# Segment sums of the opening taken by TensorE, and the layernorm of the w2 stage taken from accumulated sums and squares

## The chip, the cores and the metric

One core of a Trainium2 chip. The time is the device time of one execution in microseconds (us). A "profiled span" comes from the trace of one execution and is about 1.7 us below that execution's device time. TensorE is PE in the profile, its weight load PEld, VectorE DVE, ScalarE ACT, GpSimd POOL, SyncE SP.

## The reference, cut to what matters

```python
mod = (_silu(c) @ w_mod).reshape(1, 6, 1, -1)
sa, ca, ga, sb, cb, gb = ...                           # six vectors of 1024
h = _layernorm(x) * (1 + ca) + sa                      # x: 2048 x 1024
x = x + ga * _A_ref(h, mem0, Wq, Wk, Wv, Wo, 32)       # 64 segments of 32 rows, with a memory of 8 rows
h = _layernorm(x) * (1 + cb) + sb                      # called u in the kernel
# _B_ref(u):
g  = shifted(_gelu(_layernorm(u) @ w1))
x1 = u + g @ w2                                        # called x1b
h2 = _gelu(_layernorm(x1) @ w3) @ w4                   # the layernorm of x1 is called z
return x + gb * (x1 + h2)
```

The kernel estimates the memories of all segments from segment means (`hbar`: the sum over each segment of `h`, for the first one with the memory rows, over 40), and checks the estimate later.

## The kernel before

The opening: a tile of 128 rows is normalised (statistics on DVE, `xn` on POOL), transposed by PE into PSUM (`pt`), and evicted with scale and shift into `hh`, most of it by ACT. DVE then sums each segment out of `hh`.

```python
hsum = sb1.tile([P, KT, NSEG], F32, name="hsum")
def ln1_pair(tp_):                     # two tiles of 128 rows
    ...
    xn = xnp.tile([P, D], BF16, name="xn")                          # 3 buffers
    nc.gpsimd.tensor_scalar(xn[:], xt[:], rstd, nmr[:], ALU.mult, ALU.add)
    for kt in range(KT):
        nc.tensor.transpose(pt[:, kt, i * P:(i + 1) * P], xn[:, kt * P:(kt + 1) * P], ident[:])
    ...                                # hh = pt * (1 + ca) + sa, on DVE and ACT
    def seg_sum(s0, ns, col):
        nc.vector.tensor_reduce(hsum[:, :, s0:s0 + ns], hh[...], AX.X, ALU.add)
    ...
def g_prep():
    nc.vector.tensor_reduce(msum[:], hh[:, :, C_M0:C_M0 + M], AX.X, ALU.add)
    nc.vector.tensor_add(hsum[:, :, 0], hsum[:, :, 0], msum[:])
    nc.vector.tensor_scalar(gs["hbar"][:], hsum[:], 1.0 / (M + SEG), None, ALU.mult)
```

The w2 stage: 16 tiles of 128 rows. The tile's sum goes to memory and, normalised as `z`, through a transposing transfer into `z2a` (tiles 0 to 7) or `z2b` (8 to 15), which the w3 stage reads.

```python
def ln_act(smp, dst, src):             # bn_stats x2, bn_aggr, ve on DVE; rstd on POOL
    mean, rstd = layernorm_stats(smp, src)
    nc.vector.scalar_tensor_tensor(nmr[:], mean, -1.0, rstd, ALU.mult, ALU.mult)
    nc.scalar.activation(dst, src, ACT.Identity, bias=nmr[:], scale=rstd)
def Ba(t):
    ...
    for n2 in range(2):
        ...                            # 8 products into acc
        nc.vector.tensor_tensor(x1b[:, cs], acc[:], u[:, cs], ALU.add)
    nc.scalar.dma_start(x1b_d[ts, :], x1b[:])
    ln_act(bsm, z[:], x1b[:])
for i, u in enumerate(lagged(Ba, Bb, list(range(NTT)), lag=1)):    # Bb(t): transpose z of tile t
    u()
    ...
    if i == 14:                        # Winograd sums of z2a ("zs") and of the first w3 block ("ring")
        for f in z_sums(0):
            keep_order(f())
        w3_sums(0, keep_order)
```

A scheduler sets the order of the instructions on each engine; `keep_order` pins one behind what stands before it in the program.

Of the kernel before, what the change touches and what calls it, by code (L numbers as in the profile page):

```python
# [9 lines left out]
BF16 = mybir.dt.bfloat16  # L10
F32 = mybir.dt.float32
F16 = mybir.dt.float16
I32 = mybir.dt.int32
ACT = mybir.ActivationFunctionType
ALU = mybir.AluOpType
AX = mybir.AxisListType
# [3 lines left out]
P = 128  # L20
S = 2048
D = 1024
KT = D // P
H = 32
DH = 128
M = 8
SEG = 32
NSEG = S // SEG
# [5 lines left out]
EPS = 1e-5  # L34
# [26 lines left out]
def kernel(ctx, tc, A_x, A_mem0, A_Wq, A_Wk, A_Wv, A_Wo, A_seg_len, B_x, B_w1, B_w2, B_w3, B_w4, c, w_mod, out,  # L61
           dbg=None, force_fallback=False, no_fallback=False):
    nc = tc.nc
# [29 lines left out]
    mhalf = const.tile([P, 1], F32, name="mhalf")  # L93
    nc.vector.memset(mhalf[:], -0.5)

    saT = const.tile([P, KT], F32, name="saT")
    ca1T = const.tile([P, KT], F32, name="ca1T")
# [69 lines left out]
    def first_pass(late_hook):  # L167
# [134 lines left out]
        hh = hpool.tile([P, KT, MAIN + CONV + 1], BF16, name="hh")  # L302
        C_T0, C_M0, C_T1, C_MEM = MAIN, MAIN + 32, MAIN + 40, MAIN + 136
# [37 lines left out]
        sm = ph.enter_context(tc.tile_pool(name="ph1_sm", bufs=4, side="right"))  # L341
        sb1 = ph.enter_context(tc.tile_pool(name="ph1_sb", bufs=1, side="right"))
        pst = ph.enter_context(tc.tile_pool(name="ph1_pst", bufs=2, space=PSUM))
        wst = ph.enter_context(tc.tile_pool(name="ph1_w", bufs=6, side="right"))
        ps1 = ph.enter_context(tc.tile_pool(name="ph1_ps1", bufs=1, space=PSUM))
# [7 lines left out]
        LN_ORDER = list(range(1, NTT)) + [0]  # L353
        xts = []

        def load_x(eng, i):
            xt = xp.tile([P, D], BF16, name="xt")
            xts.append(xt)
            ins = []
            for rows, toks in p_rows(LN_ORDER[i]):  # L360
                ins.append(eng.dma_start(xt[rows, :], x2[toks, :]))
            return ins
# [13 lines left out]
        small_ps = ps1.tile([P, 512], F32, name="small_ps")  # L376
# [9 lines left out]
        for half in range(2):  # L386
            for j in range(KT):
                for kt in range(KT):
                    nc.tensor.matmul(pm[:, half * KT + j:half * KT + j + 1], lhsT=wms[half * 2 + j // 4][:, kt, (j % 4) * P:(j % 4 + 1) * P], rhs=scT[:, kt:kt + 1],
                                     start=(kt == 0), stop=(kt == KT - 1))  # L390
        nc.vector.tensor_copy(saT[:], pm[:, 0:KT])
        nc.vector.tensor_scalar(ca1T[:], pm[:, KT:2 * KT], 1.0, None, ALU.add)
        hsum = sb1.tile([P, KT, NSEG], F32, name="hsum")

        def ln1_pair(tp_):
            def f():
                pt = pst.tile([P, KT, 2 * P], BF16, name="pt")
                for i in range(2):
                    t = 2 * tp_ + i
                    xt = xts[t]  # L400
                    mean, rstd = layernorm_stats(sm, xt[:])
                    nm = sm.tile([P, 1], F32, name="ln_nm")
                    nc.vector.tensor_scalar(nm[:], mean, -1.0, None, ALU.mult)
                    nmr = sm.tile([P, 1], F32, name="ln_nmr")
                    nc.gpsimd.tensor_tensor(nmr[:], nm[:], rstd, ALU.mult)
                    xn = xnp.tile([P, D], BF16, name="xn")
                    nc.gpsimd.tensor_scalar(xn[:], xt[:], rstd, nmr[:], ALU.mult, ALU.add)
                    if t + 8 < NTT:
                        load_x(nc.gpsimd, t + 8)
                    for kt in range(KT):  # L410
                        nc.tensor.transpose(pt[:, kt, i * P:(i + 1) * P], xn[:, kt * P:(kt + 1) * P], ident[:])
                c0 = 2 * P * tp_
                pieces = [(c0, 0, 2 * P)] if tp_ < 7 else [(c0, 0, P + 32), (C_T1, P + 32, 96)]
                ndve = 4 if tp_ < 2 else 1
                for kt in range(KT):
                    for col, o, n in pieces:
                        dst = hh[:, kt, col:col + n]
                        src = pt[:, kt, o:o + n]
                        if kt < ndve:
                            nc.vector.tensor_scalar(dst, src, ca1T[:, kt:kt + 1], saT[:, kt:kt + 1], ALU.mult, ALU.add)  # L420
                        else:
                            nc.scalar.activation(dst, src, ACT.Identity, bias=saT[:, kt:kt + 1], scale=ca1T[:, kt:kt + 1])

                def seg_sum(s0, ns, col):
                    nc.vector.tensor_reduce(hsum[:, :, s0:s0 + ns], hh[:, :, col:col + ns * SEG].rearrange("p k (s j) -> p k s j", j=SEG), AX.X, ALU.add)
                if tp_ < 7:
                    seg_sum(1 + 8 * tp_, 8, c0)
                else:
                    seg_sum(57, 4, c0)
                    seg_sum(0, 1, C_T0)  # L430
                    seg_sum(61, 3, C_T1)
            return f

        def w0_unit(hp, hl, which, i):
# [11 lines left out]
        gs = {}  # L446

        def g_prep():
            msum = sb1.tile([P, KT], F32, name="msum")
            nc.vector.tensor_reduce(msum[:], hh[:, :, C_M0:C_M0 + M], AX.X, ALU.add)  # L450
            nc.vector.tensor_add(hsum[:, :, 0], hsum[:, :, 0], msum[:])
            gs["hbar"] = sb1.tile([P, KT, NSEG], BF16, name="hbar")
            nc.vector.tensor_scalar(gs["hbar"][:], hsum[:], 1.0 / (M + SEG), None, ALU.mult)
            gs["vbarT"] = sb1.tile([P, H, NSEG], BF16, name="vbarT")

        def g_v(g):
# [46 lines left out]
        for p in range(2):  # L503
            c0, c1 = slice(2 * p * CH, (2 * p + 1) * CH), slice((2 * p + 1) * CH, (2 * p + 2) * CH)
# [299 lines left out]
        for hp in range(NHP - 1):  # L804
            fill = P_units(hp + 1)
            for x in extra if hp < NHP - 2 else []:
# [5 lines left out]
                fill = merged  # L812
# [110 lines left out]
        bsm = LT.enter_context(tc.tile_pool(name="x1_sm", bufs=8))  # L923
# [53 lines left out]
        def ln_act(smp, dst, src):  # L977
            mean, rstd = layernorm_stats(smp, src)
            nmr = smp.tile([P, 1], F32, name="ln_nmr")
            nc.vector.scalar_tensor_tensor(nmr[:], mean, -1.0, rstd, ALU.mult, ALU.mult)  # L980
            nc.scalar.activation(dst, src, ACT.Identity, bias=nmr[:], scale=rstd)  # L981
# [128 lines left out]
        tp = LT2.enter_context(tc.tile_pool(name="x2_t", bufs=4))  # L1110
        bsm = LT2.enter_context(tc.tile_pool(name="x2_sm", bufs=8))

        def Ba(t):
            def f():
                ts = slice(t * P, (t + 1) * P)
                u = tp.tile([P, D], BF16, name="u2")
                nc.sync.dma_start(u[:], u_d[ts, :])
                x1b = tp.tile([P, D], F32, name="x1b")
                for n2 in range(2):
                    acc = acc_tile()  # L1120
                    for kt in range(KT):
                        o = 2 + t * P + SHIFT[kt]
                        nc.tensor.matmul(acc[:], lhsT=h1T[:, kt, o:o + P], rhs=w2s[:, kt, n2 * 512:(n2 + 1) * 512], start=(kt == 0), stop=(kt == KT - 1))  # L1123
                    cs = slice(n2 * 512, (n2 + 1) * 512)
                    nc.vector.tensor_tensor(x1b[:, cs], acc[:], u[:, cs], ALU.add)
                nc.scalar.dma_start(x1b_d[ts, :], x1b[:])
                z = tp.tile([P, D], BF16, name="z")
                ln_act(bsm, z[:], x1b[:])
                zs[t] = z
            return f  # L1130

# [906 lines left out]
```

## Time and profile before

| | before |
|---|---|
| median of 3 runs (range) | 1498.17 us (1496.54 to 1500.04) |
| profiled span | 1494.7 us |
| PE busy | 95% |
| hbar complete, first product with it | 76.2, 76.3 us |
| w2 ends, third product set of w3 begins | 1130.75, 1146.83 us |

A timeline line reads: start, duration, engine, line of the kernel, operation, what it writes and reads, shape, count; in brackets the idle time of the engine before it and what ended that. The lines of the kernel before stand in the prediction. Note that its profiled execution is the fastest of its runs.

### The profile page before, as it was taken

To read this page: it belongs to the slowest core of one execution; us is meant where nothing else is said; L and a number is where in the kernel's file an instruction comes from. 1 tells how busy PE (TensorE), PEld (TensorE's weight loads), DVE (VectorE), ACT (ScalarE), POOL (GpSimd) and SP (SyncE) were. 2 spreads that over 40 slices of the span, in tenths; PEclk is the share of its full clock that TensorE was granted. 3 is DMA by queue.
4 is the path that set the end of the run, shared out by engine and by line. 5 is a ranking of instruction groups with operands and counts; after the bars stand their busy time and mean duration, and the time that the engine had idled before them with its cause. 6 is when DMAs were issued, how large, how long until landed. Compare 5 with 4: busy or idle time off the path is not lost.

```text
span 1494.7 us, 24413 instructions
## 1 busy us (share of the span) xinstructions
PE 1425.5 (95%) x9118; PEld 750.9 (50%) x9118; DVE 924.3 (62%) x1965; ACT 665.5 (45%) x1407; POOL 359.1 (24%) x495
## 2 busy tenths in 40 slices
PE   5799999999999999999997999999997999999997
PEld 3365555565555556565553444444443444444443
DVE  5826767777677777766751354354297657575683
ACT  2715666665666665666551031123433650046400
POOL 7503100000000001000010222213012663545524
PEclk9999999999999999999998999999999999999999
DMA  9577977866778777778579999984398783477812
GB/s 318 190 283 149 187 160 185 196 148 173 162 172 179 184 162 182 158 163 182 121 197 318 299 316 352 320 231 155 107 293 243 238 271 116 147 234 239 274 43 74
DMA packets 402612, 303.47 MB, mean 203 GB/s; under 512 B 199082, under 2 KB 354730, under 8 KB 400690
## 3 DMA queue, kind: packets, MB, share of 16 engines
q1 hardware_dynamic: 363632, 238.05, 60.5%
q0 software_dynamic: 9616, 33.05, 7.4%
q10 hardware_dynamic: 29234, 30.71, 6.7%
q8 instruction: 73, 1.20, 0.3%
q14 instruction: 57, 0.47, 0.1%
HBM read 200.56 MB, written 50.63 MB: 168 GB/s over the span
## 4 chain that ended last, share of the span: by engine, by line
PE 79%; DMA 7%; DVE 5%; issue 3%; ACT 3%; POOL 2%; SPq 0%; ACTq 0%; DVEq 0%; POOLq 0%
PE acc L611 31%; PE acc L883 7%; PE bank_b L1247 6%; PE bank_b L1196 6%; PE acc L1040 4%; PE acc L1123 3%; PE acc L328 3%; PE bank_d L1196 3%; PE bank_d L1247 2%; PE bank_e L1247 2%; PE ps_o L722 2%; DMA wstream<-in_A_Wo_dram 2%; PE acc L318 2%; PE ps_s L705 2%; DMA V<-VT 2%
## 5 line engine op out<-in xcount | busy, mean ns | idle before, releaser
L883 PE MATMUL acc<-wstream,OTc 128*128 128x512 bf16 x960 | 210.3, 381 | 3.8 <-DMA OTc<-OTx_d 3.2
L611 PEld LDWEIGHTS <-T 128*128 128x128 f16 x1408 | 130.6, 97 | 119.2 <-issue 1.7
L579 ACT COPY snap<-acc 128x480 f32<-128x480 f32 x264 | 146.1, 564 | 86.7 <-PE acc L611 80.0
L611 PE MATMUL acc<-hh,T 128*128 128x480 bf16 (+1 forms) x704 | 163.1, 366 | 0.3 <-DVE VT L583 0.3
L611 PE MATMUL acc<-hs,T 128*128 128x480 f16 x704 | 157.1, 366 | 0.6 <-ACT snap L579 0.6
L883 PEld LDWEIGHTS <-OTc 128*128 128x128 bf16 x960 | 93.6, 98 | 116.6 <-DMA OTc<-OTx_d 3.7
L1196 PEld LDWEIGHTS <-ring 128*128 128x128 f16 (+1 forms) x784 | 77.5, 99 | 108.1 <-issue 15.7
L750 POOL DMA_DIRECT2D OTx_d<-OT x32 | 24.8, 775 | 422.4 <-DMA OT<-O 316.0
L709 ACT ACTIVATE E<-ps_s 99x495 bf16<-99x495 f32 (+2 forms) x160 | 87.3, 546 | 48.3 <-PE ps_s L705 47.8
L611 PE MATMUL acc<-hh,wq 128*128 128x480 bf16 x464 | 103.8, 365 | 0.0
L729 DVE TENSOR_TENSOR O<-ps_o,rin_all 99x384 bf16<-99x384 f32 (+1 forms) x192 | 97.1, 510 | 3.8
L583 DVE TENSOR_TENSOR KT<-acc,snap 128x480 bf16<-128x480 f32 x116 | 74.8, 654 | 21.5 <-PE acc L611 18.8
L1247 PEld LDWEIGHTS <-hq 128*128 128x128 bf16 (+1 forms) x560 | 54.8, 98 | 66.1
L1161 ACT COPY snap<-bank_b 128x512 f32<-128x512 f32 x72 | 40.5, 583 | 103.2 <-PE bank_b L1247 60.8
L722 PE MATMUL ps_o<-V,E 99*128 99x129 bf16 (+1 forms) x704 | 79.5, 220 | 6.2 <-DMA V<-VT 4.3
L1066 DVE TENSOR_TENSOR ring<-ring 128x1024 f16<-128x1024 bf16 (+1 forms) x64 | 78.5, 1248 | 5.6 <-PE bank_b L1247 5.2
L711 DVE TENSOR_TENSOR E<-E,maskB 99x495 bf16<-99x495 bf16 (+1 forms) x128 | 48.1, 376 | 49.2 <-ACT E L709 47.2
L722 PEld LDWEIGHTS <-E 99*128 99x128 bf16 (+1 forms) x704 | 56.2, 98 | 43.7 <-issue 4.9
L981 ACT ACTIVATE u<-x,ln_nmr,ln_rstd 128x1024 bf16<-128x1024 f32 x16 | 19.7, 1232 | 129.4 <-DVE ln_nmr L980 104.7
L110 POOL TENSOR_TENSOR ln_rstd<-ln_ve,mhalf 128x1 f32<-128x1 f32 x64 | 35.2, 550 | 172.8 <-DVE ln_ve L108 128.5
L583 DVE TENSOR_TENSOR VT<-acc,snap 128x480 bf16<-128x480 f32 x90 | 58.1, 652 | 24.9 <-PE acc L611 20.8
L1247 PE MATMUL bank_b<-ring,hq 128*128 128x512 f16 (+1 forms) x336 | 73.2, 379 | 0.0
(229 smaller groups left out, 2540.9 us busy)
## 6 DMA issues: line engine op xcount, KB each, us to landing
wstream<-in_A_Wo_dram SPq DMA_DIRECT2D x29, 1024.0 KB, 8.9
OTx_d<-OT POOLq DMA_DIRECT2D x32, 512.0 KB, 7.2
wstream<-in_B_w_dram SPq DMA_DIRECT2D x28, 512.0 KB, 5.5
ring<-in_B_w_dram SPq DMA_DIRECT2D x28, 512.0 KB, 6.1
ring<-in_B_w_dram SPq DMA_DIRECT2D x8, 1792.0 KB, 10.0
OTc<-OTx_d SPq DMA_DIRECT2D x12, 1024.0 KB, 7.5
wq<-in_A_Wq_dram SPq DMA_DIRECT2D x16, 512.0 KB, 5.4
wk<-in_A_Wk_dram SPq DMA_DIRECT2D x16, 512.0 KB, 6.7
```

The lines of the kernel that those rows point to most:

```text
L579: nc.scalar.copy(t[:], st[q][bank][:, 0:CH])
L583: nc.vector.tensor_tensor(view(d, i), chunks(st[q][bank]), chunks(st[q][s_]), ALU.add)
L611: nc.tensor.matmul(acc[:, 0:CH], lhsT=B[:, k, :], rhs=A[:, k, :], start=(j in (1, 2, 5) and k == 0), stop=(k == 3), skip_group_check=True)
L709: nc.scalar.activation(E[:rows, 0:o], ps[:rows, 0:o], ACT.Exp, scale=DH ** -0.5)
L711: nc.vector.tensor_tensor(E[:rows, 0:o], E[:rows, 0:o], mk[:rows, 0:o], ALU.mult)
L722: nc.tensor.matmul(ps[:, i, :], lhsT=state["e", h, t // 5][:k, c:c + P], rhs=V[:k, t, 0:DH + 1], start=True, stop=True)
L729: nc.vector.tensor_tensor(O[:rows, ts[0]:ts[0] + n, :], ps[:rows, 0:n, 0:DH], rin[:, :, None].to_broadcast([rows, n, DH]), ALU.mult)
L883: nc.tensor.matmul(accs[tt][:], lhsT=ot[hl // 4][:, hl % 4, tt * P:(tt + 1) * P], rhs=woc[hl // 4][:, hl % 4, :], start=(h == 0), stop=(h ...
L1040: nc.tensor.matmul(acc[:], lhsT=w1s[:, kt, ct * P:(ct + 1) * P], rhs=zT[:, kt, b * 512:(b + 1) * 512], start=(kt == 0), stop=(kt == KT - 1))
L1066: return nc.vector.tensor_tensor(dst, a, b, op)
L1196: nc.tensor.matmul(acc[:], lhsT=B[:, k, q * P:(q + 1) * P], rhs=A[:, k, :], start=(start and k == 0), stop=(k == 3), skip_group_check=True)
L1247: nc.tensor.matmul(acc[:], lhsT=L3[:, k, i * P:(i + 1) * P], rhs=R3[:, k, :], start=(start and k == 0), stop=(k == 13), skip_group_check=True)
```

## The change

Its intent: take the segment sums from DVE (10 reduces, 18 us) to PE, which sums the rows behind their transpose, by products of the same `xn` with a 128x4 matrix of ones and zeros that marks which row is of which segment (136 products; PE's weight loads rise by as many); and take the statistics of the w2 layernorm from DVE: the mean from sums that the two additions accumulate, the variance from a Square with accumulator on ACT.

```diff
-        hsum = sb1.tile([P, KT, NSEG], F32, name="hsum")
+        hsum = ps1.tile([P, KT, NSEG], F32, name="small_ps")     # PSUM, the bank of the modulation vectors
+        segs = ...                                               # 128x4: which row is of which segment
+        cm, sm_, m0 = ...                                        # (1+ca)/40, 32 sa/40, the memory rows' part
...                                                               # in ln1_pair, behind the transposes:
+                    for kt in range(KT):
+                        for dst, cols in (...):
+                            nc.tensor.matmul(hsum[:, kt, dst], lhsT=xn[:, kt * P:(kt + 1) * P], rhs=segs[:, cols], start=True, stop=True)
...
-                def seg_sum(s0, ns, col): ...                    # and its ten calls
... g_prep:
-            nc.vector.tensor_scalar(gs["hbar"][:], hsum[:], 1.0 / (M + SEG), None, ALU.mult)
+            for kt in range(KT):
+                if kt % 2:
+                    nc.vector.tensor_scalar(gs["hbar"][:, kt, :], hsum[:, kt, :], cm[:, kt:kt + 1], sm_[:, kt:kt + 1], ALU.mult, ALU.add)
+                else:
+                    nc.scalar.activation(gs["hbar"][:, kt, :], hsum[:, kt, :], ACT.Identity, bias=sm_[:, kt:kt + 1], scale=cm[:, kt:kt + 1])
+            ...                                                  # the first segment's column again, with m0
... w2:
+        def ln_sums(smp, dst, src, sums):
+            ...                                                  # nm = -(sums[0] + sums[1]) / D, on DVE
+            nc.scalar.activation(dst, src, ACT.Square, bias=nm[:], accum_out=sq[:])
+            nc.gpsimd.tensor_scalar(ve[:], sq[:], 1.0 / D, EPS, ALU.mult, ALU.add)
+            nc.gpsimd.tensor_tensor(rstd[:], ve[:], mhalf[:], ALU.pow)
+            nc.gpsimd.tensor_tensor(nmr[:], nm[:], rstd[:], ALU.mult)
+            nc.scalar.activation(dst, src, ACT.Identity, bias=nmr[:], scale=rstd[:])
-                    nc.vector.tensor_tensor(x1b[:, cs], acc[:], u[:, cs], ALU.add)
+                    nc.vector.scalar_tensor_tensor(x1b[:, cs], acc[:], 1.0, u[:, cs], ALU.mult, ALU.add, accum_out=sums[:, n2:n2 + 1])
-                ln_act(bsm, z[:], x1b[:])
+                ln_sums(bsm, z[:], x1b[:], sums)
```

More of the change, by code (lines that the diff above doesn't have):

```diff
@@ L392, in first_pass @@
         nc.vector.tensor_scalar(ca1T[:], pm[:, KT:2 * KT], 1.0, None, ALU.add)
-        hsum = sb1.tile([P, KT, NSEG], F32, name="hsum")
+        hsum = ps1.tile([P, KT, NSEG], F32, name="small_ps")
+        segs = sb1.tile([P, 4], BF16, name="segs")
+        nc.gpsimd.memset(segs[:], 1.0)
+        nc.gpsimd.affine_select(out=segs[:], in_=segs[:], pattern=[[-SEG, 4]], compare_op=ALU.is_ge, fill=0.0, base=0, channel_multiplier=1)
+        nc.gpsimd.affine_select(out=segs[:], in_=segs[:], pattern=[[SEG, 4]], compare_op=ALU.is_ge, fill=0.0, base=SEG - 1, channel_multiplier=-1)
+        cm = sb1.tile([P, KT], F32, name="cm")
+        sm_ = sb1.tile([P, KT], F32, name="sm")
+        m0 = sb1.tile([P, KT], F32, name="m0")
+        nc.vector.tensor_scalar(cm[:], ca1T[:], 1.0 / (M + SEG), None, ALU.mult)
+        nc.vector.tensor_scalar(sm_[:], saT[:], SEG / (M + SEG), None, ALU.mult)
+        nc.vector.tensor_reduce(m0[:], hh[:, :, C_M0:C_M0 + M], AX.X, ALU.add)
+        nc.vector.scalar_tensor_tensor(m0[:], m0[:], 1.0 / (M + SEG), sm_[:], ALU.mult, ALU.add)
         def ln1_pair(tp_):
@@ L411, in f @@
                         nc.tensor.transpose(pt[:, kt, i * P:(i + 1) * P], xn[:, kt * P:(kt + 1) * P], ident[:])
+                    lt = LN_ORDER[t]
+                    for kt in range(KT):
+                        for dst, cols in (((slice(4 * lt - 3, 4 * lt + 1), slice(0, 4)),) if lt else ((slice(0, 1), slice(0, 1)), (slice(61, 64), slice(1, 4)))):
+                            nc.tensor.matmul(hsum[:, kt, dst], lhsT=xn[:, kt * P:(kt + 1) * P], rhs=segs[:, cols], start=True, stop=True)
                 c0 = 2 * P * tp_
@@ L422, in f @@
                             nc.scalar.activation(dst, src, ACT.Identity, bias=saT[:, kt:kt + 1], scale=ca1T[:, kt:kt + 1])
-                def seg_sum(s0, ns, col):
-                    nc.vector.tensor_reduce(hsum[:, :, s0:s0 + ns], hh[:, :, col:col + ns * SEG].rearrange("p k (s j) -> p k s j", j=SEG), AX.X, ALU.add)
-                if tp_ < 7:
-                    seg_sum(1 + 8 * tp_, 8, c0)
-                else:
-                    seg_sum(57, 4, c0)
-                    seg_sum(0, 1, C_T0)
-                    seg_sum(61, 3, C_T1)
             return f
@@ L448, in g_prep @@
         def g_prep():
-            msum = sb1.tile([P, KT], F32, name="msum")
-            nc.vector.tensor_reduce(msum[:], hh[:, :, C_M0:C_M0 + M], AX.X, ALU.add)
-            nc.vector.tensor_add(hsum[:, :, 0], hsum[:, :, 0], msum[:])
             gs["hbar"] = sb1.tile([P, KT, NSEG], BF16, name="hbar")
-            nc.vector.tensor_scalar(gs["hbar"][:], hsum[:], 1.0 / (M + SEG), None, ALU.mult)
+            for kt in range(KT):
[3 more added lines that the diff above has]
+                    nc.scalar.activation(gs["hbar"][:, kt, :], hsum[:, kt, :], ACT.Identity, bias=sm_[:, kt:kt + 1], scale=cm[:, kt:kt + 1])
+            first = sb1.tile([P, KT], F32, name="first")
+            nc.vector.tensor_tensor(first[:], hsum[:, :, 0], cm[:], ALU.mult)
+            nc.vector.tensor_tensor(gs["hbar"][:, :, 0], first[:], m0[:], ALU.add)
             gs["vbarT"] = sb1.tile([P, H, NSEG], BF16, name="vbarT")
@@ L1111, in first_pass @@
         bsm = LT2.enter_context(tc.tile_pool(name="x2_sm", bufs=8))
+        def ln_sums(smp, dst, src, sums):
+            nm = smp.tile([P, 1], F32, name="ln_nm")
+            nc.vector.tensor_tensor(nm[:], sums[:, 0:1], sums[:, 1:2], ALU.add)
+            nc.vector.tensor_scalar(nm[:], nm[:], -1.0 / D, None, ALU.mult)
+            sq = smp.tile([P, 1], F32, name="ln_sq")
+            nc.scalar.activation(dst, src, ACT.Square, bias=nm[:], accum_out=sq[:])
+            ve = smp.tile([P, 1], F32, name="ln_ve")
+            nc.gpsimd.tensor_scalar(ve[:], sq[:], 1.0 / D, EPS, ALU.mult, ALU.add)
+            rstd = smp.tile([P, 1], F32, name="ln_rstd")
+            nc.gpsimd.tensor_tensor(rstd[:], ve[:], mhalf[:], ALU.pow)
+            nmr = smp.tile([P, 1], F32, name="ln_nmr")
+            nc.gpsimd.tensor_tensor(nmr[:], nm[:], rstd[:], ALU.mult)
+            nc.scalar.activation(dst, src, ACT.Identity, bias=nmr[:], scale=rstd[:])
         def Ba(t):
@@ L1118, in f @@
                 x1b = tp.tile([P, D], F32, name="x1b")
+                sums = bsm.tile([P, 2], F32, name="ln_sums")
                 for n2 in range(2):
```

## The prediction

> **What bounds the kernel now.** I read the page first, then the windows of the two stages that the change touches, then the waits and the timelines around their edges.
>
> ```profile
> PE 1425.5 (95%) x9118; PEld 750.9 (50%) x9118; DVE 924.3 (62%) x1965; ACT 665.5 (45%) x1407; POOL 359.1 (24%) x495
> PE   5799999999999999999997999999997999999997
> PE 79%; DMA 7%; DVE 5%; issue 3%; ACT 3%; POOL 2%; SPq 0%; ACTq 0%; DVEq 0%; POOLq 0%
> ```
>
> TensorE is busy for 95% and carries 79% of the chain that ended last. Only where its digit falls below 9 can a change to another engine gain much: the first two slices (the opening) and the slice with a 7 near 1130 us, the end of the w2 stage. The change touches just these two. A steady stretch of the w2 stage, its end, and two stretches of the w3 start, in the windows view (length, then PE, PEld, DVE, ACT, POOL busy, clock, DMA share, GB/s):
>
> ```profile
> 1105.00:1120.00 15.00, 15.00 (x71) 6.76 (x69) 13.93 (x32) 5.17 (x5) 2.74 (x5) 1.00 1.20 286
> 1141.00:1147.00 6.00, 0.17 (x1) 0.10 (x1) 1.89 (x3) 1.92 (x4) 0.00 (x0) 0.74 0.44 114
> 1147.00:1151.00 4.00, 4.00 (x11) 1.42 (x10) 1.19 (x2) 1.87 (x4) 2.53 (x2) 0.53 0.90 270
> ```
>
> In the stage DVE is 93% busy, but PE is 100% busy: taking work off DVE there is worth nothing until the stage ends. PE's gaps, from the PE timeline (start, duration, what, idle before and its releaser), opening first:
>
> ```profile
> 64.46 0.62 PE L411 MATMUL pt<-ident,xn 128*128 128x128 bf16 x8 [1.05 <-POOL xn L407]
> 66.94 1.78 PE L318 MATMUL acc<-hh,wk 128*128 128x480 bf16 x8
> 76.34 3.20 PE L465 MATMUL acc<-hbar,wchunk 128*128 128x64 bf16 x64 [7.61 <-DVE hbar L453]
> ...
> 1132.01 1.89 PE L1196 MATMUL bank_b<-z2a,ring 128*128 128x512 bf16 x8 [1.27 <-DMA x1b_d<-x1b]
> 1137.06 1.90 PE L1196 MATMUL bank_b<-zs,ring 128*128 128x512 f16 x8 [1.44 <-DVE ring L1066]
> 1146.83 3.57 PE L1196 MATMUL bank_b<-zs,ring 128*128 128x512 f16 x8 [6.14 <-ACT snap L1161]
> ```
>
> So 7.6 us are lost waiting for hbar and 8.9 us (1.27 + 1.44 + 6.14) around the w2/w3 edge. What leads to each, from the DVE and ACT timelines:
>
> ```profile
> 63.77 2.29 DVE L425 TENSOR_REDUCE hsum<-hh 128x64 f32<-128x2048 bf16 x1 [3.13 <-ACT hh L422]
> 72.30 2.41 DVE L425 TENSOR_REDUCE hsum<-hh 128x32 f32<-128x1024 bf16 x3 [1.35 <-ACT hh L422]
> 75.77 0.42 DVE L453 TENSOR_SCALAR hbar<-hsum 128x512 bf16<-128x512 f32 x1
> ...
> 1139.61 1.24 ACT L981 ACTIVATE z<-x1b,ln_nmr,ln_rstd 128x1024 bf16<-128x1024 f32 x1 [5.09 <-DVE ln_nmr L980]
> 1144.35 1.29 DVE L1204 TENSOR_TENSOR join<-bank_e,snap 128x512 f32<-128x512 f32 x2 [4.83 <-DMA z2b<-z]
> ```
>
> hbar needs sums of hh, which needs ScalarE's last eviction; and the first join of w3 waits for the transpose of the last w2 tile's z (the join buffer takes over freed memory), so the last tile's whole layernorm is a serial path.
>
> [...] The opening's 128x1 products run 32 in 0.87 us (18.36 to 19.23), 27 ns each. [...] After the 6.14 us gap the window shows 0.53, and the first 16 matmuls take 5.4 us (1146.83 to 1152.20) in place of 3.5: about 1.9 us lost besides the wait. [...] z took 1.24. [...] I use 1.25 with its accumulator output.
>
> **Part 1, the segment sums.** Removed: ten tensor_reduce on DVE, 18.3 us in all (seven of 2.27, three smaller). Added on PE: 15 tiles x 8 plus 16 = 136 products of at most 4 columns, 136 x 27 ns = 3.7 us, about 0.25 per tile. hbar becomes eight small scale-and-shift pieces, four each on ACT and DVE, some 0.3 us each. The gain is not 18.3: DVE is only one supplier. I walked the order of the changed kernel with the durations of the trace.
>
> The start gets worse. The new sums reuse the PSUM bank of the modulation vectors, so the first cannot start before these are copied out (19.65 us), and xn has three buffers: the fourth xn now waits for the first tile's sums as well. POOL's fixed order puts this xn behind the masks (18.25 + 4.35 = 22.6, done at 23.8). Transposes of tile 3 move from 19.7 to 23.9, and the first projection from 21.6 to about 25.0.
>
> Then DVE gives back: without 4.46 us of reduces before tile 4's statistics, these begin at 26.2 and xn of tile 4 is done at about 31.0, against 32.7. POOL sets the pace up to tile 9, with the distances of the old trace (2.65, 3.0, 2.15, 3.5) and 2.0 for the last, whose order changed: 44.3. In the new order PE then has 21 projections, 2 tiles, 24, 2 tiles, 24, 2 tiles: 69 x 0.203 = 14.0, plus 6 x (0.44 + 0.25) = 4.1, from about 45.1. The last sums end at T' = 63.4; the last transposes ended at 65.1 before. PE is then the supplier that binds.
>
> From T': ACT does one hbar piece, 14 evictions (4.8) and three casts, then the other three pieces, at T'+7.8. DVE, in its order, has four Winograd sums (4.3), waits for the evictions to T'+5.3, then 1.07 + 1.07 + 0.3 + 1.07, two pieces and two 128x8 operations: hbar complete at T'+9.6 = 73.0, against 76.2. So hbar no longer waits for a reduce, but the scheduler put its last pieces behind the Winograd sums. **Gain 3.2 us.** After that PE is full to 113 us in the same order in both kernels, so the shift should persist.
>
> **Part 2, LN of w2.** Removed per tile: two bn_stats (0.69 each), an aggregate (0.21), ve and nmr (0.15, 0.16): 1.9 of DVE's 3.3 us. Added: accumulators on the two additions (I leave them at 0.70) and two 128x1 operations (0.3). DVE comes to 1.7 us of the 3.45 us that PE needs per tile (55.4 / 16). ACT gets Square + Identity, 1.25 + 1.24, plus 0.34 of DMA issue and short waits: 3.1 of 3.45. It fits. In ACT's order the identity of tile t stands behind the store of tile t+1, so z comes about 5.1 us after the addition, not 3.3; only the transposes see this. PE stays at 55.4 us: no gain within the stage.
>
> At its end E (1130.75 before) the order puts the last addition behind all four z sums and one ring sum. DVE: addition of tile 14's second half to E-2.7, nm to E-2.4, z sum to E-1.3, first half of tile 15 to E-0.6, three z sums to E+2.8, ring to E+3.4, second half to E+4.1, two ring sums, nm at E+5.5. The first w3 matmul needs this PSUM bank: E+4.2, 2.9 later than before. ACT: store, Identity 14 to E+5.7, Square 15 to E+7.0; POOL ve, rstd (0.55), nmr to E+8.1; Identity 15 to E+9.4; the transpose of 3.06 to E+12.5, join at E+12.9 against E+13.6. PE's earlier w3 work (6.9 us, 2 more at a low clock, and one wait for ACT at E+9.9) ends near E+13.1, so its late start hides behind the join. Two gelus and a snap later the third product set begins at E+15.3, against E+16.1: 0.8. The gap before it shrinks from 6.1 to about 2 us, so the clock penalty of 1.9 us after it falls away. **Gain 2.5 us**, with the clock its softest part.
>
> Sum: 3.2 + 2.5 = 5.7; 1498.17 - 5.7 = **1492.5 us**.
>
> **Rivals.** (a) *DVE was the bound of the opening*: then nearly all that the reduces took between 24 and 72 us comes back, 8 to 10 us, and the total is near 1486. For it: POOL waits for DVE's statistics between 49 and 62 (1.1 to 2.4 us each). Against: tile 3's new wait, and PE's own 18 us after tile 9. (b) *The early blockage costs more than is won back*: PE stands behind tile 3 for 3.5 us and the clock may drop; if tile 4 comes no earlier than 32.7, hbar comes at 75 or later and part 1 is worth 0 to 1: near 1495. (c) *ScalarE becomes the bound of w2*: if Square, identity, issue and waits exceed 3.45 by 0.3, 16 tiles add 5 us to the last z and none to PE until the edge: near 1497 to 1499. Against it are the 0.35 us of slack per tile. (d) *The late last addition shows*: if PE's w3 start is what counts, part 2 loses up to 3 us: near 1498.
>
> **Range and chances.** Each part is within about 4 us of my figure, and the before runs spread by 3.5 us; 8 times in 10 I expect 1487.5 to 1498.0. A gain or loss of 2% (30 us) is more than all gaps of the two places together (about 16.5 us plus the projection stalls), so within 2% gets 0.98, the others 0.01 each.
>
> **What would show it.** In the trace after: the transposes of tile 3 near 24 and the first projection near 25; the small sums at some 27 ns each; hbar's wait on PE of about 4.7 us, ending at 72 to 74, with DVE's Winograd sums just before; w2 still 55.4 us with DVE near 50% and ACT near 75%; the first w3 matmul some 4 us after w2's last, the join still released by the z transpose, and a clock near 1.0 in the third product set. I am wrong if hbar ends before 69 or after 76, if PE idles inside w2, or if any stage between 120 and 1070 us changes length by more than 2 us.

Passages for which no trace of this case stands are cut, and the cuts are marked. The 1.25 us "with its accumulator output" is for Square, an estimate: no trace then showed a Square, and the Identity of z, of the same 128x1024, took 1.24. And that a gap of about 2 us leaves the clock high is an estimate from the trace of before: there eight products of w3 took 1.89 and 1.90 us behind waits of 1.27 and 1.44 us, and 3.57 behind one of 6.14 (clock 0.50 from 1143.9 to 1150.8 us).

## The result, and the profile after

| | before | after |
|---|---|---|
| median (range), 4 runs each on one chip | 1499.11 (1496.54 to 1500.12) | 1490.35 us (1489.56 to 1491.53) |
| profiled span | 1494.7 | 1488.7 us |

The ratio is 0.9945, 95% interval 0.9928 to 0.9962: the same at 2%, 8 us faster by the ratio. A ratio is the mean time of one kernel's fast runs over the mean of the other's in the same rounds, so it is not quite the ratio of the medians. A second series below gave 0.9956.

From the page of the changed kernel, the engine totals: DVE fell from 62 to 60%, ACT rose from 45 to 46%.

```profile
PE 1422.2 (96%) x9198; PEld 754.4 (51%) x9254; DVE 898.1 (60%) x1946; ACT 685.3 (46%) x1443; POOL 379.1 (25%) x530
```

**The opening.** The PE timeline after: the transposes of tile 3, the first projection, the last segment sums, and the first products with hbar.

```profile
23.64 1.03 PE L423 MATMUL pt<-ident,xn 128*128 128x128 bf16 x8 [1.45 <-POOL xn L419]
25.18 0.56 PE L318 MATMUL acc<-hh,wq 128*128 128x480 bf16 x1 [0.31 <-DVE hh L436]
...
62.40 0.54 PE L427 MATMUL small_ps<-segs,xn 128*128 128x1 bf16 x16
...
73.26 3.57 PE L477 MATMUL acc<-hbar,wchunk 128*128 128x64 bf16 x64 [5.43 <-DVE hbar L465]
76.64 2.62 PE L318 MATMUL acc<-hh,wq 128*128 128x480 bf16 x8
```

The prediction had 23.9 and 25.0 for the first two places, 63.4 for the last sums (62.9 here), 73.0 for hbar (73.1). The sums cost what it said: eight of a later tile take 0.20 us, 25 ns each. The last two lines are what it did not have: the 64 products take 3.57 us, the eight that follow 2.62, against 3.20 and 1.78 in the kernel before. The wait is shorter, but more of the low clock falls on work: both traces have one stretch of 6.8 us at a clock of 0.50 there (72.1 to 78.9 us before, 71.5 to 78.3 after), and PE works in 2.6 us of it before, in 5.1 after. DVE between the last sums and hbar:

```profile
63.42 0.34 DVE L460 TENSOR_SCALAR hbar<-small_ps,cm,sm 128x64 bf16<-128x64 f32 x1 [0.22 <-ACT hbar L462]
63.69 1.15 DVE L519 TENSOR_TENSOR hs<-hh 128x1920 f16<-128x1920 bf16 x1
...
70.59 1.15 DVE L521 TENSOR_TENSOR hs<-hh,hs 128x1920 f16<-128x1920 bf16 x1
```

The sums are all there at 62.9, but seven of the eight Winograd sums (7 x 1.15 = 8.0 us) stand among the pieces of hbar.

**The w2 stage and its end.** Windows of the kernel after (length, then PE, PEld, DVE, ACT, POOL busy, clock, DMA share, GB/s): the steady stage, and the first product sets of w3.

```profile
1105.00:1120.00 15.00, 14.95 (x70) 6.78 (x70) 7.54 (x26) 9.84 (x13) 3.93 (x13) 1.00 1.05 282
1135.30:1141.00 5.70, 5.68 (x16) 2.12 (x17) 1.24 (x4) 4.46 (x6) 1.40 (x4) 0.60 0.92 220
1146.40:1150.00 3.60, 3.52 (x17) 1.63 (x17) 2.06 (x3) 2.75 (x6) 2.56 (x2) 1.00 0.80 257
```

DVE fell from 13.93 to 7.54 us in the same 15 us, PE is full in both. The timelines of PE, ACT and DVE at the edge (w2's last product ends at 1131.0):

```profile
1135.32 3.57 PE L1224 MATMUL bank_b<-z2a,ring 128*128 128x512 bf16 x8 [4.32 <-POOL ln_rstd L1135]
1139.38 1.24 ACT L1138 ACTIVATE z<-x1b,ln_nmr,ln_rstd 128x1024 bf16<-128x1024 f32 x1 [0.75 <-POOL ln_nmr L1137]
1144.01 1.29 DVE L1232 TENSOR_TENSOR join<-bank_e,snap 128x512 f32<-128x512 f32 x2 [7.43 <-PE bank_d L1224]
1146.48 1.89 PE L1224 MATMUL bank_b<-zs,ring 128*128 128x512 f16 x8 [1.86 <-ACT snap L1189]
```

From the end of w2: first w3 product at 4.3 us (predicted 4.2), join at 13.0 (12.9), third set at 15.5 (15.3), now at a clock of 1.00 (third window). The low clock did not vanish, it moved to the first sets (0.60 in the second window), where the wait for the join hides it. At the join the timeline names PE as the releaser. The view of the chain (--critical) names the transpose of the last z, as the prediction had it; the join begins 0.3 us after it lands:

```profile
1140.65 3.04 DMA z2b<-z
```

**Where the time went.** I matched ScalarE's instructions of two traces in order, and took for each kernel how many us earlier than in the first profile of before the same instruction starts (minus: later), and, separately, the tail: the time from DVE's last instruction to the end of the span. The later rows are the experiments'.

```
profile          72   81   622   660   718   744  1065  1200  1335   tail    span
before            0    0     0     0     0     0     0     0     0    6.6  1494.7
same_before    -0.2 -0.8  -0.9  -0.8  -0.9  -0.9  -1.0  -1.2  -1.2    6.3  1495.5
after           3.4  1.9   1.9   0.5   0.0  -0.5  -0.3   2.3   3.8    4.5  1488.7
same_after      2.7  1.8   1.8   0.5   0.0  -2.4  -1.9   0.6   0.8    4.5  1491.7
p1_sums_only    4.0  3.2   3.2   1.9   1.4  -1.3  -1.4  -1.1  -0.9    4.5  1493.5
p2_ln_only      0.0 -0.3  -0.8  -0.8  -0.8  -0.8  -0.3   2.2   2.4    4.6  1490.3
before_pad136  -0.6 -1.0  -1.0  -2.3  -2.3  -3.0  -4.3  -4.7  -4.7    6.4  1499.1
after_pad120    2.6  2.1   1.9   1.9   1.3   1.3   1.9   4.4   3.1    4.5  1489.5
rows2           3.6  2.2   2.0   1.0   0.4  -0.2  -1.9   0.6   0.8    4.4  1491.6
edge_first      3.8  2.0   2.0   0.7   0.2  -0.4  -0.3   1.8   3.5    4.7  1489.2
early_bn        4.2  2.8   2.6   1.2   0.6  -1.8  -1.8  -1.7  -1.7    4.7  1494.5
hbar_first      3.7  9.0   8.9   7.6   7.0   6.3   6.6   9.1   7.7    4.8  1485.2
best            3.8  9.1   9.1   8.0   8.0   7.3   8.1   8.8   8.8    5.1  1484.4
hbar_pad120     3.5  8.9   9.3   9.3   8.8   8.8   7.2   9.7  10.0    4.4  1482.4
```

Read the row "after". ScalarE is 3.4 us early at its last cast before hbar (hbar itself is 3.1 early). At 81 the lead is 1.9, as the products behind hbar take 1.2 us more at the low clock. It stays level to 622, and all of it is lost by 718. Then 2.5 us are won at the w2/w3 edge, 1.7 at 1318 us, and 2.1 in the tail. The lead at 1335 and the tail together, 5.9, is near the prediction's 5.7, but it is made of other parts. That is what the experiments are about.

### The profile page after: what moved, and what is told of

It reads as the page before. It is cut to its first block, busy times and chain, and to the rows that moved or that the text cites. A ratio compares the mean times of both kernels' runs of the same rounds, so it can differ in the third digit from the quotient of the medians.

```text
span 1488.7 us, 24706 instructions
## 1 busy us (share of the span) xinstructions
PE 1422.2 (96%) x9198; PEld 754.4 (51%) x9254; DVE 898.1 (60%) x1946; ACT 685.3 (46%) x1443; POOL 379.1 (25%) x530
## 4 chain that ended last, share of the span: by engine, by line
PE 78%; DMA 5%; DVE 5%; issue 4%; POOL 3%; ACT 3%; ACTq 0%; SPq 0%; DVEq 0%; POOLq 0%
PE acc L623 29%; PE acc L895 7%; PE bank_b L1275 6%; PE bank_b L1224 6%; PE acc L1052 4%; PE acc L328 3%; PE bank_d L1224 3%; PE acc L1151 3%; PE acc L318 3%; PE bank_e L1275 2%; PE bank_d L1275 2%; PE ps_o L734 2%; DMA wstream<-in_A_Wo_dram 2%; PE ps_s L717 2%; PE bank_e L1224 1%
## 5 line engine op out<-in xcount | busy, mean ns | idle before, releaser
L1078 DVE TENSOR_TENSOR ring<-ring 128x1024 f16<-128x1024 bf16 (+1 forms) x64 | 85.6, 1357 | 5.3 <-PE bank_b L1275 4.8
L739 ACT ACTIVATE O<-ps_o,rin_all 99x128 bf16<-99x128 f32 x192 | 56.7, 369 | 36.8 <-DVE rin_all L736 36.4
L736 DVE RECIPROCAL rin_all<-ps_o 99x3 f32<-99x3 f32 (+2 forms) x256 | 42.7, 171 | 50.5 <-PE ps_o L734 49.8
L1275 PE MATMUL bank_b<-ring,hq 128*128 128x512 f16 (+1 forms) x334 | 73.1, 379 | 0.1
```

The costliest lines, as they stand in the source:

```text
L739: nc.scalar.mul(O[:rows, t, :], ps[:rows, i, 0:DH], rin[:, i:i + 1])
L1078: return nc.vector.tensor_tensor(dst, a, b, op)
L1275: nc.tensor.matmul(acc[:], lhsT=L3[:, k, i * P:(i + 1) * P], rhs=R3[:, k, :], start=(start and k == 0), stop=(k == 13), skip_group_check=True)
```

## The experiments

Twelve kernels, five timed runs each (four of the last); all gave correct results. They ran in four series, each on one chip and with its own runs of before: the four of the first group; the two pads with hbar_first and edge_first; early_bn, rows2 and best; hbar_pad120.

### The parts alone, and both kernels once more

Edits: `p1_sums_only` is the change without its w2 part, `p2_ln_only` without its opening, `same_after` and `same_before` are the two kernels unaltered.

> Only the segment sums of the opening are changed; w2 keeps its old layernorm. In the two profiles at hand the opening is 3.1 us ahead when hbar is complete, 1.9 us ahead from 81 to 630 us, and level at 720 us. Theory A (the opening's gain carries to the end, the loss between 630 and 720 us was the chance timing of transfers): 1.5 to 3 us faster than the kernel before, ratio 0.998 to 0.999, and this trace again shows hbar complete near 73 with 1.9 us carried past 720. Theory B (the transposing transfers of the attention stages set the time and take the gain back in any run): within 0.7 us of before, level at 720 us again.

> Only the layernorm of the w2 stage is changed; the opening keeps its reduces. Theory A: 2.5 us faster than before (the third product set of w3 begins about 2.3 to 2.6 us earlier relative to the end of w2, because the clock does not drop there), ratio near 0.998; the two parts then add up to what the whole change gives. Theory B (all of the gain is in this part): 5 us or more, ratio 0.9965 or less, and the same as the whole change. In both w2 itself stays at 55.4 us of PE and ScalarE's period there at 3.59 us.

> The changed kernel once more, unaltered, for a second profile. If the 2.3 us lost between 630 and 720 us, the 1.7 us won at 1318 us (eight products in 1.89 in place of 3.52 us after the same 3.25 us wait) and the 1.5 us won in the tail after the last product belong to the change, they are in this profile too, within 0.3 us. If they are chance, at least one of them is missing or of another size. Ratio 0.993 to 0.997.

> The kernel before under a second name, a null test: ratio 0.999 to 1.001, and the spread of its second profile from the first shows how far two executions of one program differ stage by stage. If 1318 us shows eight products in 1.9 us here, the clock loss there was chance and not of the kernel before.

| | median us | ratio to before (1498.81) | 95% interval |
|---|---|---|---|
| p1_sums_only | 1494.40 | 0.9976 | 0.9962 to 0.9989 |
| p2_ln_only | 1492.11 | 0.9967 | 0.9953 to 0.9981 |
| same_after | 1491.97 | 0.9956 | 0.9942 to 0.9969 |
| same_before | 1497.53 | 0.9996 | 0.9983 to 1.001 |

The null test holds. Three things follow from the table of leads.

First, of the six profiles at hand, the three with the segment sums all lose between 622 and 744 us, at the same places, 632, 676 and 721 us, and the three without them do not. It is not chance, so theory A was wrong there; nor is all of the gain in the other part, as B had it.

Second, the tail is 4.5 or 4.6 us in all four profiles with anything changed, 6.3 to 6.6 in both of before. So each part alone shows it, and the whole has it once: by the ratios the parts give 3.6 + 4.9 = 8.5 us, the whole 6.6, and 8.5 less one tail of 2 is 6.5. The intervals are about 2 us either way, so this agrees rather than proves. p2_ln_only came out between its two theories, as neither had the tail: 2.5 us at the edge and 2 in the tail.

Third, the gain at 1318 us was chance. In the PE timelines, before and then after:

```profile
1317.91 3.52 PE L1196 MATMUL bank_b<-zs,ring 128*128 128x512 f16 x8 [3.25 <-ACT snap L1161]
```
```profile
1315.78 1.89 PE L1224 MATMUL bank_b<-zs,ring 128*128 128x512 f16 x8 [3.24 <-ACT snap L1189]
```

The same wait of 3.25 us, once with a low clock behind it (0.50 from 1318.0 to 1321.4 us) and once without (1.00). Ahead of the end of the run, the records of the granted clock show low stretches of 3.4 or 6.8 us only. At this wait same_before, same_after and p2_ln_only have one of 3.4, after and edge_first none, after_pad120 and hbar_first one of 6.8. So the length of the wait alone does not decide it: what follows this wait of 3.25 us differs between two executions of the same kernel (after and same_after). What does decide it no run here shows.

### What takes the opening's gain back: an instruction count

In the DMA view around 630 us (issue, count, KB, us from issue to landing), before and then after:

```profile
V<-VT SPq DMA_TRANSPOSE x1, 5.5
rows_d<-row_a POOLq DMA_DIRECT2D x1, 1.0 KB, 2.5
```
```profile
q8 instruction: 1, 0.02, 0.8%
V<-VT SPq DMA_TRANSPOSE x1, 7.4
rows_d<-row_a POOLq DMA_DIRECT2D x1, 1.0 KB, 4.4
```

Two transfers, a transpose that PE waits for and a 1 KB write that DVE waits for, land 1.9 us later. The page calls the queue q8 "instruction"; I take it for TensorE's instruction fetch: 73 packets of 16 KB in the whole run before, 74 after, which at PE's 18,236 instructions (matmuls and weight loads) is 250 to a packet on average, and the padding of PE below moves them. After, one of them runs from 629.56 to 630.48 us. Of the 32 packets of the write, 30 have started by 629.43; the last two run at 630.47 and 630.49, when the fetch is over. The segment sums add 136 products and 136 weight loads, 272 instructions. In the kernel before, the block nearest to this place starts at 636.0 us; the one after, with the lead of 1.9 us added, stands at 631.5 of that time, so 4.6 us earlier, and falls on the two transfers. My theory: the count of instructions sets this place. To test it without the change:

```diff
+        for _ in range(136):           # 120 in after_pad120; TensorE is idle here, nothing reads the result
+            nc.tensor.matmul(small_ps[0:8, 256:264], lhsT=ident[:, 0:8], rhs=ident[:, 0:8], start=True, stop=True)
         pc = pst.tile([P, KT, 2 * P], BF16, name="pt")
```

That 512 more instructions put the blocks back where they were was an assumption; the landings below test it.

> The kernel before with 136 tiny products (an 8-column weight load and an 8-column product each) put on TensorE at the very start, where it is idle; nothing reads them. They add just as many TensorE instructions as the segment sums do (272). Theory F (the loss of the opening's gain between 630 and 745 us comes from where the 16 KB blocks of TensorE's instruction fetch fall, and the count of instructions sets that): a block is fetched about 4.5 us earlier in the program, DVE again waits 1.7 us for the write of row_a near 634 us and the kernel falls 1.3 us behind the first profile of before there, and another 0.5 to 2 us at 721 us; at 620 us it is still level within 1 us. Theory G (the loss comes from the shifted start of the stages, whatever the count): no such wait, level with before throughout. In time: F 1.5 to 3 us slower than before, G the same within 0.7 us.

> The changed kernel with 120 such products at the start: 272 + 240 = 512 TensorE instructions more than before, [...] so the blocks fall where they fell in the kernel before. Theory F: the waits at 632 and (in size) at 721 us are those of before again; the lead of 1.9 us at 620 us is still at least 1.2 us at 745 us, and the kernel is 1 to 3 us faster than the changed kernel, ratio to before 0.992 to 0.995. Theory G: the lead is lost by 745 us as in all three profiles with the segment sums, ratio 0.995 to 0.997.

before_pad136: 1500.96 us, ratio 1.0015 (1.0001 to 1.0028), 2.2 us slower than before, for 272 instructions in idle time. It is 1.0 behind at 622 us and 2.3 at 660. Its waits around 630 us (engine, line, waited for: us, times, longest) are those of the changed kernel, and so is the landing:

```profile
DVE row_a L265 <- DMA rows_d<-row_a: 1.7, 1, 1.7
PE ps_o L724 <- DMA V<-VT: 0.9, 1, 0.9
```
```profile
V<-VT SPq DMA_TRANSPOSE x1, 7.4
rows_d<-row_a POOLq DMA_DIRECT2D x1, 1.0 KB, 4.4
```

after_pad120: 1491.21 us, ratio 0.9951 (0.9937 to 0.9965). The landings are 5.4 and 2.5 us again:

```profile
V<-VT SPq DMA_TRANSPOSE x1, 5.4
rows_d<-row_a POOLq DMA_DIRECT2D x1, 1.0 KB, 2.5
```

Nothing is lost at 632 or 721, and the lead of 1.9 us is still 1.9 at 1065. Theory F holds for those two places in both directions. The 0.5 us at 676 us stays, which a count of PE alone need not touch: in that window the page's other instruction queue, q14 (57 packets of 8 KB in the whole run, before and after), has two blocks after and none before. That this is its cause was not tested, but all fourteen traces fit it. With each kernel's lead added, so in the time of before, a q14 block starts at 675.3 to 675.4 us in the nine profiles that lose there, and at 678.7 to 678.9 in the five that do not; one of these is best, which has the segment sums and loses nothing (8.0 at 660 and 718). In time the run is only as fast as the changed kernel, not 1 to 3 us faster: the clock at 1318 us took 1.2 us from this profile and had given 1.7 to the first one of after, so this size of gain cannot be read from the times here.

```diff
-                            st["a"] = pool.tile([P, 256], F32, name="row_a")
+                            st["a"] = pool.tile([P, 256], F32, name="row_a", bufs=2)
```

> The changed kernel with two buffers for row_a in place of one, nothing else. If DVE's wait for the write of the row before (1.66 us at 631.7 us, the last of 32 pieces of that write late behind a 16 KB block of instruction fetch) is what costs 1.3 us there, that wait is gone and the lead of 1.85 us at 620 us is still 1.85 at 660; the losses at 676 (0.5) and 721 us (0.5 to 2.4) stay, as they wait for other transfers. 1.3 us faster than the changed kernel, which a median alone can hardly show; the trace decides. If the wait moves to the next row or another transfer, the lead at 660 us is 0.5 again.

rows2: 1492.41 us, ratio 0.9958 (0.9945 to 0.9972). A miss, and a useful one. DVE no longer waits for the write, but PE does for the transpose, 0.93 us as in the changed kernel (DVE, then PE):

```profile
629.72 0.34 DVE L265 TENSOR_SCALAR row_a<-row_w,sc 128x256 f32<-128x256 bf16 x1
```
```profile
631.82 0.33 PE L734 MATMUL ps_o<-V,E 104*128 104x129 bf16 x3 [0.93 <-DMA V<-VT]
```

Both transfers landed late behind the same block, after 7.4 and 4.4 us. I had named the one with the longer wait; the other ends later, and 1.1 us of lead are lost all the same.

### What holds hbar

```diff
             for kt in range(KT):
-                if kt % 2:
-                    nc.vector.tensor_scalar(gs["hbar"][:, kt, :], ...)
-                else:
-                    nc.scalar.activation(gs["hbar"][:, kt, :], ...)
+                nc.vector.tensor_scalar(gs["hbar"][:, kt, :], ...)
             ...
+            gs["last"] = nc.vector.tensor_tensor(gs["hbar"][:, :, 0], first[:], m0[:], ALU.add)
...                                     # each of the eight Winograd sums w:
+                tc.add_manual_dep(w.ins, gs["last"].ins.name, ...NoSync...)     # order on DVE, no wait
```

> The changed kernel with all eight pieces of hbar on DVE and the eight Winograd sums ordered behind them. If DVE's order is what made hbar late (the sums of the segments end near 63 us, hbar only at 73), hbar is complete at 65 to 66 us, before TensorE's last projection at 67.7; the wait of 5.4 us on TensorE and the cold clock after it (1.2 us) go, and 81 us of the kernel before comes 7 to 8.5 us earlier than in it, in place of 1.9. The time is 4 to 6.5 us below the changed kernel's. If instead the evictions on ScalarE or a transfer held hbar, the wait stays above 3 us and the gain is under 2 us.

hbar_first: 1486.90 us, ratio 0.9919 (0.9906 to 0.9933), 4 to 5.5 us below the changed kernel's two series by the ratios. DVE, then PE:

```profile
62.81 2.10 DVE L459 TENSOR_SCALAR hbar<-small_ps,cm,sm 128x64 bf16<-128x64 f32 x8
```
```profile
68.48 2.03 PE L474 MATMUL acc<-hbar,wchunk 128*128 128x64 bf16 x64 [0.96 <-ACT VT L122]
```

Two small operations follow, and hbar is complete at 65.2 in place of 73.1. PE waits 0.96 us, for an eviction on ACT, and the 64 products take 2.03 us in place of 3.57, at the pace of the later groups of 32 (1.10). The lead at 81 us is 9.0, half a us above the range I gave. So this edit was worth 7 us, more than twice what the change itself won in the opening. The edit puts the pieces on one engine and orders them first at once, so it does not say how much of that the hand-over between ACT and DVE cost. In the changed kernel the two engines wait for each other's pieces three times (0.74 and 0.92 us on ACT, 0.47 on DVE); here the eight pieces take 2.1 us together.

### What holds the w3 start

```diff
-            if i == 14:
+            if i == 15:                # z and ring sums behind the last tile's additions
                 for f in z_sums(0):
```

> The changed kernel with the four z sums and three ring sums ordered behind the last tile's additions, one unit later. If the last tile's layernorm holds the join and starts late only because its addition stands behind the z sums, the first w3 product starts about 1 us after the last of w2 (4.3 now), the identity of tile 15 ends near 6.5 us after it (9.6 now), the first join comes near 9.7 (13.0 now) and the third product set near 12.2 (15.5 now): 3 us faster than the changed kernel. If the ring and z sums were what counted, the second set waits until 7 us, and less than 1 us is won.

edge_first: 1492.76 us, ratio 0.9961 (0.9948 to 0.9975): no gain, a miss. The first w3 product does come 0.9 us after w2, but the last Identity ends 10.0 us after w2, not 6.5, the join comes at 13.4 and the third set at 15.9. POOL's three steps for tile 14:

```profile
1132.88 0.52 POOL L1133 TENSOR_SCALAR ln_ve<-ln_sq 128x1 f32<-128x1 f32 x1 [2.49 <-ACT z L1131]
1133.49 1.53 POOL L1135 TENSOR_TENSOR ln_rstd<-ln_ve,mhalf 128x1 f32<-128x1 f32 x1
1135.10 0.70 POOL L1137 TENSOR_TENSOR ln_nmr<-ln_nm,ln_rstd 128x1 f32<-128x1 f32 x1
```

In the steady stage these take 0.19, 0.55 and 0.19 us. Here DVE's z sums run from 1132.14 to 1136.88, and Identity of tile 14 waits on ACT until 1135.83, with tile 15's Square behind it. In this trace only POOL steps under such sums are stretched, and the first and the third of these end at 1133.40 and 1135.80, each 0.05 us after one of the sums (1133.35 and 1135.75). What the two engines share there no run here shows. So I had moved the z sums from in front of the layernorm to beside it, where they cost the same.

```diff
-            if i == 14: ...            # the z and ring sums
+            if i == 9: w3_sums(0, keep_order); early = z_sums(0)
+            if 10 <= i < 14: keep_order(early[i - 10]())
...                                     # and for t >= 14 the plain addition and ln_act, as in the kernel before
```

> The changed kernel with the sums for w3 taken earlier (three ring sums at tile 9, one z sum behind each of tiles 10 to 13, where DVE now has over 1 us free per tile) and the old layernorm for tiles 14 and 15 only. Theory (the last z, and with it the first join and the third product set, is held by a serial path: Square, read of its sum, three GpSimd steps, Identity, and these steps are stretched by DVE's z sums): the first w3 product starts about 1 us after the last of w2, the identity of tile 15 ends near 4.2 us after it (9.6 in the changed kernel), the join comes near 7.5 (13.0) and the third product set near 10 (15.5), with at most one cold window: 4 to 6 us faster than the changed kernel from there on. If PE stalls inside w2 now, DVE's slack was smaller than I think; w2's 55.4 us on PE would grow. If the transpose or the memory of the join holds the third set whatever the identity does, it stays above 14.

early_bn: 1494.25 us, ratio 0.9972 (0.9958 to 0.9985), 2 to 4 us slower than the changed kernel by the ratios. Its interval overlaps that of same_after (0.9942 to 0.9969), so the times alone do not show a loss. Between 1065 and 1200 us the trace shows no gain (a lead of -1.8 at 1065 and -1.7 at 1200): a miss with two reasons. DVE, ACT, then the DMA issue on SP:

```profile
1119.64 1.23 DVE L1078 TENSOR_TENSOR zs<-z2a 128x2048 f16<-128x2048 bf16 x1 [3.06 <-DMA z2a<-z]
```
```profile
1135.62 2.36 ACT L993 ACTIVATE z<-x1b,ln_nmr,ln_rstd 128x1024 bf16<-128x1024 f32 x2
```
```profile
1136.13 7.70 SPq L1167 DMA_TRANSPOSE z2b<-z  x3
```

The z sums need z2a, and its last tile had landed only at 1119.6: DVE stood 3.06 us in its fixed order, which set back the layernorm of the tiles behind. And though the last Identity ends at 1138.0, 5.5 us after w2 (in place of 9.6), three transposes stood one behind the other from 1136.1 on, about 3.3 us each, and the join came at 1146.1, 13.6 after. In this trace the transposes are serial, so an earlier last z should help only if the two before it come earlier too; no run tried that. w2 stayed at 55.42 us on PE. The edge stays as the change left it.

### Together

`best` joins hbar_first, early_bn and rows2; `hbar_pad120` is hbar_first with the 120 tiny products.

> hbar_first, early_bn and rows2 together. If the three are separate, the lead over before is 9 us at 81 us, 8.4 at 697 (0.5 lost at 676), 6 to 8 at 1065, 5 us more behind the w3 edge, and with the shorter tail 13 to 16 us in all: 1482.5 to 1485.5, ratio 0.989 to 0.991, so still within 2%. A chance cold window at the start of the second pair of w3 may take 1.7 to 2.9 us of it.

best: 1486.25 us, ratio 0.9922 (0.9908 to 0.9935), the same as hbar_first and below what I expected, as two of its three parts gain nothing: it leads by 9.1 us at 622, and the edge gives 0.7 in place of 2.5.

> hbar_first with the 120 tiny products at the start[...]. Theory F once more, with another lead: hbar_first led by 8.9 us at 620 us and lost 1.3 at 632, 0.5 at 676 and 0.7 at 721 us. Here the first and the third loss should be gone: a lead of about 9 at 660, 8.4 at 700 and 8.4 at 745 us, and 1.5 to 2.5 us less time than hbar_first: 1484 to 1486, ratio 0.990 to 0.992. If the losses return, the alignment of after_pad120 was chance.

hbar_pad120: 1484.51 us, ratio 0.9901 (0.9884 to 0.9918), the fastest of all. The lead is 9.3 us at 622 and 660, 8.8 at 718 and 744: again only the 0.5 at 676 is lost there, where hbar_first lost 2.6 in all. Between 744 and 1065 it loses another 1.6, as rows2 does (1.7) and before_pad136 (1.3); what takes that was not looked into. It ran in another series than hbar_first, so the 2 us between them are within the two intervals; the trace shows the landings of before a second time (5.5 and 2.5 us), from another lead.

## Why the prediction was right or wrong

The predicted time, 1492.5 us, is 2.1 us above the first median and 0.5 above the second, and the class was right. Step by step:

- **Two slips in the working.** The row of PE's digits has five places below 9, not three: there is a second 7 near 800 us, and one in the last slice, where the 2.1 us of the tail were to come from. And 45.1 + 14.0 + 4.1 is 63.2, not 63.4; 0.8 + 1.9 is 2.7, not 2.5. Neither sum matters.
- **The opening up to hbar: right.** Tile 3 at 23.6, first projection 25.2, hbar at 73.1, 3.1 us earlier (3.2 predicted), and for the reason given: PE had its sums, and DVE's Winograd sums stood among the pieces. I took that order as given. hbar_first shows that placing the pieces ahead was the largest thing to win there.
- **"The shift should persist": wrong, twice.** Of the 3.1 us, 1.2 went to the low clock (0.50 for 6.8 us) behind hbar's wait of 5.4 us. I had counted the wait and not what follows it, though I had done so at the other edge. Its size differs between profiles: in after_pad120 the low stretch there is 3.4 us, not 6.8, and ScalarE's lead falls by 0.5 (2.6 to 2.1), not 1.5. The rest went at 632, 676 and 721 us, where the prediction saw only that PE is full in the same order. By its own test (a stage between 120 and 1070 us that changes by over 2 us) it was wrong there: the stretch from 622 to 744 grew by 2.3 and 4.2 us in the two profiles (in the second a low-clock stretch of 3.4 us follows the wait at 721). At 632 and 721 the cause is the place of the instruction blocks, shown by padding in both directions; at 676 a block of q14 fits and was not tested. Part 1 was worth 3 us where it acted and less than nothing at 1065 us.
- **The layernorm stage: right for PE, wrong for ACT.** w2 takes 55.42 us on PE in both, as said. "3.1 of 3.45. It fits" is the term that failed: Square took 1.13 us and the read of its sum 0.19 (1.25 estimated for both), Identity 1.24 as before, but POOL's three steps stand between them, and the next Square stands behind the waiting Identity. ACT waits 1.22 us in each tile and its period is 3.59; it is busy for 66%, not near 75%. The two ACT groups and the wait:

```profile
1126.83 1.24 ACT L1138 ACTIVATE z<-x1b,ln_nmr,ln_rstd 128x1024 bf16<-128x1024 f32 x1 [1.22 <-POOL ln_nmr L1137]
1127.97 1.13 ACT L1131 ACTIVATE z<-x1b,ln_nm 128x1024 bf16<-128x1024 f32 x1
1129.01 0.19 ACT L1131 ACTIVATION_READ_ACCUMULATOR z<-x1b,ln_nm 128x1 f32 x1
```

  ACT lags by 0.14 us a tile, which PE hides until the edge. That is rival (c) in its first half; its second half, 5 us more at the end, did not come.
- **The w2/w3 edge: right.** 2.5 us predicted, 2.5 measured (from 0.3 behind to 2.3 ahead), with the first product, the join and the third set each within 0.2 us. The clock penalty did not disappear, it moved under a wait that was there anyway, as the working had it ("2 more at a low clock").
- **Not predicted at all: the tail,** 2.1 us shorter here after DVE's last instruction. It is 4.4 to 5.1 us in every kernel whose other engines' instruction streams were changed, against 6.6, and 6.4 where only PE's was. In the DMA view of the tail, before and then after:

```profile
q14 instruction: 4, 0.03, 1.9%
```
```profile
q14 instruction: 3, 0.02, 1.8%
```

  The blocks there come about 2.2 us apart, one fewer after. That the instruction count decides it fits all rows, but no run changed that alone: it stays argued.

So the sum was right in part because unforeseen losses (1.2 by the clock, 2.3 by 744 us) met unforeseen gains (2.1 in the tail, 1.7 by the clock at 1318). Of the rivals, (a) was out: removing 18 us from DVE gave 3. (b) was out too, the early stop at tile 3 happened and was made good before the last tiles. The late first w3 product, rival (d), is real and hidden. What stays open: the profile of before is one of its fastest runs and I did not find which stage makes its others slower.

## What to carry to other kernels

Ask what stands in front of an instruction on its own engine before asking how fast its inputs come: ten small instructions, put on one engine and ahead of eight long ones, gained more than moving 18 us of work off the engine. Follow a gain through the whole trace, with a second profile of both kernels, before believing the difference of two totals. And an instruction count is an input like any other: when stages far from the change shift, compare where instruction fetch falls (here one block of 0.92 us delayed two transfers by 1.9 us), and test with padding that does nothing else.
